# Leaky-form weight conversion, reciprocals by transposes, and one attention form for batches 1 to 3 in a fused attention and two-MLP kernel

## The chip, the cores and the metric

The kernel runs on one core of a Trainium2 chip. The metric is the device time of one execution in microseconds. The engines are TensorE (PE, with its weight loads as PEld), VectorE (DVE), ScalarE (ACT), GpSimd (POOL) and SyncE (SP), which issues most of the DMAs.

## The reference, cut to what matters

```python
def _attn_ref(q, k, v, g_q, g_k):            # (4, 12, 448, 64) each
    q_n, k_n = rmsnorm(q, g_q), rmsnorm(k, g_k)
    scores = np.matmul(q_n, k_n.transpose(0, 1, 3, 2)) / np.sqrt(64)
    attn = np.exp(scores - np.max(scores, axis=-1, keepdims=True))
    attn = attn / (np.sum(attn, axis=-1, keepdims=True) + 1e-09)
    return np.matmul(attn, v)

x = attn_out.transpose(0, 2, 1, 3).reshape(1792, 768)
x = (1 / (1 + np.exp(-(x @ w_gate)))) * (x @ w_val) @ w_out      # 768 -> 1536 -> 768
out = np.maximum(x @ w_in2, 0) ** 2 @ w_out2                     # 768 -> 2048 -> 768
```

The five weight matrices arrive as 64-bit floats, everything else as 32-bit floats.

## The kernel before

The four batches of 448 tokens pass one after the other through both MLPs (`sweep`, line 519). One pass walks over 68 weight blocks of 128x768: 24 of gate and value in turn, 12 of `w_out`, 16 of `w_in2`, 16 of `w_out2`. A product of 32-bit accuracy is made of three products of rounded operands, high by high, high by low and low by high (`mm3`, lines 508 to 512; lines 615 to 617 in the last stage). Only the first twelve blocks of the pass over batch 0 are multiplied in plain 32-bit form (line 539). High and low part of a block are made by `w_split`: ScalarE rounds (line 164), VectorE subtracts (line 165).

In the pass over batch 0 each block is first made from 64-bit words by `w_conv`: ScalarE scales the upper word, read as a 32-bit float (line 137), VectorE masks the sign bit in place (140), shifts the scaled word left by three and joins the sign (144), and joins the three top bits of the lower word (146). GpSimd then stores the 32-bit block to device memory (153), and the later passes load it from there (120). Three raw buffers and three converted ones make the ring; `w_ahead` sets how far loads, conversions and splits run ahead.

Batch 0's attention runs before the first pass, in an order written out by hand (`prologue`), and its end overlaps the first plain blocks. The attention of batch b+1 runs inside the pass over batch b: `slots_of` makes a list of small steps, which the main loop spreads evenly over the pass. Batches 0 and 1 use plain 32-bit products: scores per query chunk (`s_mm`), a maximum over two heads (`s_max`, line 268), exponentials, transposes of the probabilities (`c_mm`), products with V (`pv_mm`, line 313), and the reciprocals of the sums brought into the transposed layout by eight products with the identity per head pair (line 318). Batches 2 and 3 use the split form, the functions whose names end in 2: query and key are split into high and low parts (`a_hi`, `a_lo`), the halves that the other head's partitions need are copied by DMA (`a_dma`), scores take two products (line 398), the probabilities are normalised before the transposes (lines 425 to 430), split again behind them (`c_hi`, `c_lo`), and multiplied by a split V (lines 470, 472). A half is one head with two of the four query chunks; a batch has 24.

A scheduler then orders the instructions of each engine, and each engine runs its own queue in that order.

Of the kernel before, what the change touches and what calls it, by code (L numbers as in the profile page):

```python
# [8 lines left out]
F32 = mybir.dt.float32  # L9
# [8 lines left out]
def attention_moe_moe2_kernel(  # L18
# [104 lines left out]
    def w_conv():  # L123
# [183 lines left out]
    def pv_mm(st, o, rt):  # L307
# [330 lines left out]
    def slots_of(b):  # L638
# [5 lines left out]
        def do_s(key, c0):  # L644
            st = pairs[key]
            for c in (c0, c0 + 1):
                s_mm(st, c, att_tile())
            for c in (c0, c0 + 1):
                s_max(st, c)
                mid.append((s_exp, (st, c)))  # L650
            if c0 == 2:
                later(1, s_rec, st)

        def do_c(key, c):
            st = pairs[key]
            ps = att_tile().rearrange("p a (k c) -> p a k c", k=NF + 1)
            c_mm(st, c, ps[:, 0], ps[:, 1])
            c_copy(st, c, (act, act))

        def do_pv(key):  # L660
            st = pairs[key]
            ps = att_tile()
            pv_mm(st, ps[:, 0, :S], ps[:, 1, :S])
            for fn in (x_rec, x_sum, x_hi):
                mid.append((fn, (st,)))
            later(1, x_lo, st)
            later(1, lambda: pairs.pop(key))

        def do_a(key):
# [278 lines left out]
```

## Time and profile before

| | |
|---|---|
| median of three runs | 1309.39 us (1307.68 to 1309.93) |
| the profiled execution | 1309.2 us, span 1307.1 us |
| TensorE busy | 1284.9 us, 98% |
| VectorE busy | 938.4 us, 72% |
| ScalarE busy | 781.7 us, 60% |
| GpSimd busy | 130.3 us, 10% |

Shares are of the span. TensorE's matmuls are pipelined and their ends are modelled, so its busy time includes the tail of each; a stretch at 100% can still hold waits shorter than that tail. The span has the start-up (to 87 us), the pass over batch 0 (to 433), those over batches 1 (to 750), 2 (to 1047) and 3.

### The profile page before, as it was taken

To read this page: it belongs to the slowest core of one execution; us is meant where nothing else is said; L and a number is where in the kernel's file an instruction comes from. 1 tells how busy PE (TensorE), PEld (TensorE's weight loads), DVE (VectorE), ACT (ScalarE), POOL (GpSimd) and SP (SyncE) were. 2 spreads that over 40 slices of the span, in tenths; PEclk is the share of its full clock that TensorE was granted. 3 is DMA by queue.
4 is the path that set the end of the run, shared out by engine and by line. 5 is a ranking of instruction groups with operands and counts; after the bars stand their busy time and mean duration, and the time that the engine had idled before them with its cause. 6 is when DMAs were issued, how large, how long until landed. Compare 5 with 4: busy or idle time off the path is not lost.

```text
span 1307.1 us, 19338 instructions
## 1 busy us (share of the span) xinstructions
PE 1284.9 (98%) x6899; PEld 1120.1 (86%) x6899; DVE 938.4 (72%) x1643; ACT 781.7 (60%) x1600; POOL 130.3 (10%) x100
## 2 busy tenths in 40 slices
PE   8999999999899999999999999999999999999998
PEld 6554488788697999999999999999999999999998
DVE  6876999899898678768986478877897544435521
ACT  5764687568666678656664477765676455524421
POOL 3201214210221001000010000100010000000000
PEclk9999999999899999999999999999999999999999
DMA  5426897787788434333343533434324343333331
GB/s 144 103 76 216 273 292 246 252 270 218 245 232 273 130 113 121 105 114 107 107 113 105 146 97 110 125 100 114 99 86 121 116 127 109 109 109 109 108 114 46
DMA packets 155807, 189.62 MB, mean 145 GB/s; under 512 B 76096, under 2 KB 119616, under 8 KB 155712
## 3 DMA queue, kind: packets, MB, share of 16 engines
q1 hardware_dynamic: 148416, 161.19, 43.0%
q0 software_dynamic: 5440, 26.74, 5.0%
q8 instruction: 55, 0.90, 0.3%
q10 hardware_dynamic: 1856, 0.46, 0.2%
q14 instruction: 40, 0.33, 0.1%
HBM read 150.60 MB, written 32.24 MB: 140 GB/s over the span
## 4 chain that ended last, share of the span: by engine, by line
PE 73%; issue 10%; DVE 7%; DMA 4%; ACT 4%; POOL 2%; POOLq 0%; ACTq 0%; SPq 0%; DVEq 0%
PE acc L510 15%; PE acc L511 15%; PE acc L512 15%; PE acc L617 5%; PE acc L615 5%; PE acc L616 5%; PE att L398 3%; PE att L439 2%; DMA w<-wraw 2%; PE att L470 2%; POOL ms L232 1%; DVE nm L268 1%; PE att L472 1%; ACT p L280 1%; PE acc L313 1%
## 5 line engine op out<-in xcount | busy, mean ns | idle before, releaser
L165 DVE TENSOR_TENSOR wsp<-wraw,wsp 128x768 fp32r<-128x768 f32 x260 | 248.0, 954 | 130.8 <-ACT wsp L164 125.9
L510 PE MATMUL acc<-xy,wsp 128*128 128x448 f32 x888 | 326.7, 368 | 0.2 <-ACT rl L592 0.2
L512 PE MATMUL acc<-xy,wsp 128*128 128x448 f32 x888 | 326.1, 368 | 0.0
L511 PE MATMUL acc<-xy,wsp 128*128 128x448 f32 x888 | 325.9, 367 | 0.0
L164 ACT CAST wsp<-wraw 128x768 fp32r<-128x768 f32 x260 | 216.6, 834 | 130.9 <-PE acc L617 64.7
L512 PEld LDWEIGHTS acc<-xy,wsp 128*128 128x128 f32 x888 | 166.9, 188 | 16.1 <-issue 2.7
L510 PEld LDWEIGHTS acc<-xy,wsp 128*128 128x128 f32 x888 | 166.8, 188 | 16.1 <-issue 0.9
L511 PEld LDWEIGHTS acc<-xy,wsp 128*128 128x128 f32 x888 | 166.9, 188 | 15.0 <-issue 1.5
L232 POOL TENSOR_TENSOR ms<-ms,mhalf 112x16 f32<-112x16 f32 (+1 forms) x25 | 91.1, 3648 | 577.1 <-DVE ms L231 486.8
L616 PE MATMUL acc<-wsp,rb 128*128 128x384 f32 x384 | 129.2, 336 | 0.0
L617 PE MATMUL acc<-wsp,rb 128*128 128x384 f32 x384 | 129.0, 336 | 0.0
L615 PE MATMUL acc<-wsp,rb 128*128 128x384 f32 x384 | 128.8, 335 | 0.0
L510 PE MATMUL acc<-hb,wsp 128*128 128x448 f32 x288 | 106.2, 369 | 0.0
L511 PE MATMUL acc<-hb,wsp 128*128 128x448 f32 x288 | 105.5, 367 | 0.0
L512 PE MATMUL acc<-hb,wsp 128*128 128x448 f32 x288 | 105.5, 367 | 0.0
L417 ACT ACTIVATE p<-att,nm,ms 112x448 f32<-112x448 f32 x96 | 68.8, 724 | 34.7 <-DVE nm L408 34.5
L137 ACT ACTIVATE wraw<-raw 128x768 f32<-128x768 f32 x56 | 51.5, 920 | 51.8 <-DMA w<-wraw 27.8
L592 ACT ACTIVATE rl<-acc 128x448 f32<-128x448 f32 x64 | 35.0, 547 | 70.7 <-PE acc L512 69.9
L280 ACT ACTIVATE p<-att,nm 112x448 f32<-112x448 f32 x88 | 55.3, 639 | 33.7 <-DVE nm L268 32.3
L617 PEld LDWEIGHTS acc<-wsp,rb 128*128 128x128 f32 x384 | 72.1, 188 | 1.6 <-issue 1.3
L616 PEld LDWEIGHTS acc<-wsp,rb 128*128 128x128 f32 x384 | 72.1, 188 | 0.8 <-issue 0.7
L615 PEld LDWEIGHTS acc<-wsp,rb 128*128 128x128 f32 x384 | 72.1, 188 | 0.2
(136 smaller groups left out, 2167.7 us busy)
## 6 DMA issues: line engine op xcount, KB each, us to landing
wraw<-w SPq DMA_DIRECT2D x204, 384.0 KB, 3.0
w<-wraw POOLq DMA_DIRECT2D x56, 384.0 KB, 6.0
raw<-in_moe_w_out_dram SPq DMA_DIRECT2D x28, 768.0 KB, 5.4
raw<-in_moe_w_in_dram SPq DMA_DIRECT2D x16, 768.0 KB, 6.6
raw<-in_moe_w_gate_dram SPq DMA_DIRECT2D x12, 768.0 KB, 6.8
raw<-in_moe_w_val_dram SPq DMA_DIRECT2D x12, 768.0 KB, 6.1
out_dram<-ob SPq DMA_DIRECT2D x28, 192.0 KB, 2.9
qs<-qs SPq DMA_DIRECT2D x24, 224.0 KB, 3.0
```

What stands on the lines that cost most here:

```text
L137: size = nc.scalar.activation(out=t, in_=hi.bitcast(F32), func=AF.Copy, scale=2.0 ** -112)
L164: nc.scalar.copy(out=sp[:, 0], in_=t)
L165: nc.vector.tensor_tensor(out=sp[:, 1], in0=t, in1=sp[:, 0].bitcast(F32), op=ALU.subtract)
L232: nc.gpsimd.tensor_tensor(out=ms, in0=ms, in1=mhalf[:QR, 0:ms.shape[1]], op=ALU.pow)
L280: nc.scalar.activation(out=p[:, e], in_=ps[:QR, e, :S], func=AF.Exp, bias=nm[:, e:e + 1], scale=st["rq"][:, c, e:e + 1] if "rq" in st else ...
L417: nc.scalar.activation(out=p[:, i * (S + TAIL):i * (S + TAIL) + S], in_=ps[:QR, i, :S], func=AF.Exp, bias=nm[:, i:i + 1], scale=rq[:, 2 * ...
L510: nc.tensor.matmul(out=o, lhsT=wh, rhs=xh, start=start, stop=False)
L511: nc.tensor.matmul(out=o, lhsT=wh, rhs=xl, start=False, stop=False)
L512: nc.tensor.matmul(out=o, lhsT=wl, rhs=xh, start=False, stop=stop)
L615: nc.tensor.matmul(out=o, lhsT=rh, rhs=wh, start=(k1 == 0), stop=False)
L616: nc.tensor.matmul(out=o, lhsT=rh, rhs=wl, start=False, stop=False)
L617: nc.tensor.matmul(out=o, lhsT=rl, rhs=wh, start=False, stop=(k1 == K2 - 1))
```

## The change

Three edits. In `w_conv` ScalarE applies Prelu with slope 2^32 for negative values in place of a Copy: the slope adds 32 to the exponent of a negative word, and the shift by three moves that bit into the sign's place. VectorE then takes the three top bits of the lower word and joins them to the shifted word: two instructions instead of three. In `s_rec` GpSimd spreads the reciprocals over 64 columns per head, and four transposes replace the eight products of line 318; this form now serves batch 0 alone. In `slots_of` the plain branch goes, and batch 1 takes the split form, as do its first loads in the prologue.

```diff
-        size = nc.scalar.activation(out=t, in_=hi.bitcast(F32), func=AF.Copy, scale=2.0 ** -112)
+        size = nc.scalar.activation(
+            out=t, in_=hi.bitcast(F32), func=AF.Prelu, scale=2.0 ** -112, alpha=2.0 ** 32)
...
-        sign = nc.vector.tensor_scalar(
-            out=hi, in0=hi, scalar1=-(2 ** 31), scalar2=None, op0=ALU.bitwise_and)
+        low3 = nc.vector.tensor_scalar(
+            out=hi, in0=lo, scalar1=29, scalar2=None, op0=ALU.logical_shift_right)
...
         nc.vector.scalar_tensor_tensor(
             out=ti, in0=ti, scalar=3, in1=hi, op0=ALU.logical_shift_left, op1=ALU.bitwise_or)
-        nc.vector.scalar_tensor_tensor(
-            out=ti, in0=lo, scalar=29, in1=ti, op0=ALU.logical_shift_right, op1=ALU.bitwise_or)
...
         nc.vector.reciprocal(out=su, in_=su)
+        sb = st["sb"] = tmp_p.tile([128, 512], F32, tag="tmp", name="sb")[:QR].rearrange(
+            "p (c e d) -> p c e d", c=QC, e=2)
+        nc.gpsimd.tensor_copy(out=sb, in_=su.unsqueeze(3).to_broadcast([QR, QC, 2, D]))
...
         for c in range(QC):
-            for e in range(2):
-                nc.tensor.matmul(
-                    out=rt[e * D:(e + 1) * D, c * QR:(c + 1) * QR],
-                    lhsT=st["su"][:, c, e:e + 1].to_broadcast([QR, D]), rhs=ident[:QR, :QR],
-                    start=True, stop=True)
+            nc.tensor.transpose(
+                rt[:, c * QR:(c + 1) * QR], sb[:, c].rearrange("p e d -> p (e d)"), ident[:QR, :QR])
...
-        if b > 1:
-            for h in range(H):
...
         if b == 1:
-            add(lambda: do_stat((1, 0)))
+            add(lambda: do_stat((1, 0)), lambda: do_v((1, 0)))
             for _ in range(3):
                 add(lambda: None)
-            add(lambda: do_a((1, 0)))
-        for hp in range(HP):
-            key, nk = (b, hp), nxt(b, hp)
...
+            add(lambda: do_a2((1, 0)))
+        for h in range(H):
+            key, e = (b, h // 2), h % 2
...
```

The rest of `slots_of` behind this is the loop that batches 2 and 3 had, unchanged. How the scheduler's order moves, at three places:

VectorE, in the pass over batch 0, right behind the sixth gate-and-value pair's first product on VectorE (`L556`) in the kernel before; raw and wraw are the conversion's buffers, wsp the split block, su the sums of a softmax, nm its negated maxima:

```order
L556 TENSOR_TENSOR e<-acc,e 128x448
L287 TENSOR_SCALAR su<-su 112x8
L165 TENSOR_TENSOR wsp<-wraw,wsp 128x768
L146 SCALAR_TENSOR_TENSOR wraw<-raw_1432,wraw 128x768
L557 SCALAR_TENSOR_TENSOR e<-t,e 128x448
L288 RECIPROCAL su<-su 112x8
L140 TENSOR_SCALAR raw_1466<-raw_1466 128x768
L144 SCALAR_TENSOR_TENSOR wraw<-wraw,raw_1466 128x768
L165 TENSOR_TENSOR wsp<-wraw,wsp 128x768
L146 SCALAR_TENSOR_TENSOR wraw<-raw_1466,wraw 128x768
L559 TENSOR_TENSOR hb<-e,hb 128x448
```

The same stretch of that queue in the changed kernel, some instructions further on (`L141`, `L145` and `L164` are the two conversion steps and the split there; p and parts are the probabilities before and behind their transposes):

```order
L425 TENSOR_SCALAR su_1382<-su_1382 112x2
L145 SCALAR_TENSOR_TENSOR wraw<-wraw,raw_1563 128x768
L426 RECIPROCAL su_1382<-su_1382 112x2
L164 TENSOR_TENSOR wsp<-wraw,wsp 128x768
L430 TENSOR_SCALAR p<-p,su_1382 112x448
L430 TENSOR_SCALAR p<-p,su_1382 112x384
L430 TENSOR_SCALAR p<-p,su_1382 112x64
L457 TENSOR_TENSOR parts<-att,parts 128x3x224
L461 TENSOR_TENSOR parts<-att,parts 64x112 x2
L141 TENSOR_SCALAR raw_1614<-raw_1614 128x768
L405 TENSOR_REDUCE nm<-att 112x2
```

A conversion has lost its third row, and what stands between two conversions is now the normalising, splitting and maxima of the split attention.

TensorE, in the plain blocks (`L539`), before:

```order
L539 MATMUL acc<-xplain,wsp 128x448 x25
L244 MATMUL att<-ident,qk 128x112 x4
L539 MATMUL acc<-xplain,wsp 128x448 x6
L244 MATMUL att<-ident,qk 128x112 x4
L539 MATMUL acc<-xplain,wsp 128x448 x11
L262 MATMUL att<-kq 112x448 x4
L539 MATMUL acc<-xplain,wsp 128x448 x11
L295 MATMUL att<-ident,p 128x112 x7
L539 MATMUL acc<-xplain,wsp 128x448 x2
L295 MATMUL att<-ident,p 128x112 x7
```

and now (`L243` and `L398` prepare and multiply batch 1's first queries and keys):

```order
L539 MATMUL acc<-xplain,wsp 128x448 x33
L243 MATMUL att<-ident,qk 128x112 x4
L539 MATMUL acc<-xplain,wsp 128x448 x26
L398 MATMUL att<-ks,qs 112x448 x8
L539 MATMUL acc<-xplain,wsp 128x448 x8
L510 MATMUL acc<-xy_232,wsp 128x448
```

The two transposes of query and key have become one group, the plain score products have become two groups of four split ones, and the first transposes of probabilities have left the plain blocks.

TensorE again, where the pass over batch 0 meets that over batch 1 in the changed kernel (`L512` belongs to batch 1's first block):

```order
L512 MATMUL acc<-xy_1048,wsp 128x448
L439 MATMUL att<-ident,p 128x112 x6
L440 MATMUL att<-ident,p 128x112
L470 MATMUL att<-parts,vs 128x448
L472 MATMUL att<-parts,vs 128x448
L470 MATMUL att<-parts,vs 128x448
L472 MATMUL att<-parts,vs 128x448
L470 MATMUL att<-parts,vs 128x448
L472 MATMUL att<-parts,vs 128x448
L470 MATMUL att<-parts,vs 128x448
L398 MATMUL att<-ks,qs 112x448 x4
L510 MATMUL acc<-xy_1048,wsp 128x448
```

In the kernel before no attention step of batch 1 stands behind the first product of the pass over batch 1; here the last two steps with V and the transposes ahead of the last do, the products with V right behind these transposes.

## Rows read from the trace of the kernel before

**Rows 1.** windows: stretch, us, busy (count) of PE PEld DVE ACT POOL, PEclk, DMA share, GB/s

```profile
87.20:155.60 68.40, 67.07 (x231) 34.23 (x229) 50.73 (x76) 36.28 (x70) 13.13 (x14) 1.00 0.66 217
155.60:216.80 61.20, 57.65 (x314) 47.67 (x313) 59.82 (x87) 48.40 (x97) 12.74 (x14) 1.00 0.83 263
276.20:363.70 87.50, 83.87 (x443) 67.78 (x442) 80.78 (x127) 62.19 (x131) 12.23 (x18) 0.96 0.79 242
749.70:1047.30 297.60, 297.60 (x1613) 277.09 (x1612) 232.95 (x461) 193.56 (x409) 19.00 (x5) 1.00 0.38 109
1047.30:1307.10 259.80, 256.53 (x1323) 242.30 (x1320) 105.92 (x155) 105.37 (x188) 0.00 (x0) 1.00 0.34 104
```

**Rows 2.** timeline of DVE, three marking rows (start us, us, engine, line)

```profile
165.19 0.62 DVE L556 TENSOR_TENSOR e<-acc,e 128x448 f32<-128x448 f32 x1
...
367.56 0.61 DVE L593 TENSOR_TENSOR r<-rl 128x448 f32<-128x448 f32 x1
...
441.05 0.62 DVE L556 TENSOR_TENSOR e<-acc,e 128x448 f32<-128x448 f32 x1 [1.70 <-ACT p L417]
```

**Rows 3.** timeline of PE, start-up, plain blocks and first split block

```profile
56.19 3.23 PE L313 MATMUL acc<-pt,v 128*64 128x448 f32 x16
59.25 0.94 PE L318 MATMUL acc<-ident,su 112*64 112x112 f32 x16
...
131.69 1.76 PE L262 MATMUL att<-kq 64*112 64x448 f32 x8
...
141.75 0.84 PE L295 MATMUL att<-ident,p 112*128 112x112 f32 x7
...
155.58 0.71 PE L510 MATMUL acc<-xy,wsp 128*128 128x448 f32 x1
```

**Rows 4.** timeline of DVE, a full queue in the pass over batch 0

```profile
197.34 0.97 DVE L144 SCALAR_TENSOR_TENSOR wraw<-wraw,raw 128x768 int32<-128x768 int32 x1
198.21 0.58 DVE L140 TENSOR_SCALAR raw<-raw 128x768 int32<-128x768 int32 x1
198.68 0.64 DVE L331 TENSOR_TENSOR rs<-att,rs 128x448 f32<-128x448 f32 x1
199.21 0.97 DVE L146 SCALAR_TENSOR_TENSOR wraw<-raw,wraw 128x768 int32<-128x768 int32 x1
```

**Rows 5.** groups by form, 155 to 430 us (busy us, mean ns | idle before)

```profile
L137 ACT ACTIVATE wraw<-raw 128x768 f32<-128x768 f32 x52 | 47.8, 919 | 48.9 <-DMA w<-wraw 27.8 <-DVE wsp L165 15.0 <-issue 2.5
...
L268 DVE TENSOR_REDUCE nm<-att 112x2 f32<-112x896 f32 x22 | 23.8, 1083 | 0.0
...
L226 DVE TENSOR_REDUCE ms<-sq 112x8 f32<-112x512 f32 x10 | 6.8, 682 | 0.0
```

**Rows 6.** chain that ended last, one piece (start us, us, what)

```profile
436.47 0.82 PE att L398 x4
```

**Rows 7.** timeline of POOL, in the start-up and in stretch B

```profile
32.06 2.90 POOL L232 TENSOR_TENSOR ms<-ms,mhalf 112x16 f32<-112x16 f32 x1 [9.52 <-DVE ms L231]
...
222.16 7.65 POOL L232 TENSOR_TENSOR ms<-ms,mhalf 112x16 f32<-112x16 f32 x1 [0.72 <-DVE ms L231]
```

**Rows 8.** groups by form, 430 to 720 us, pass over batch 1

```profile
L457 DVE TENSOR_TENSOR parts<-att,parts 128x672 fp32r<-128x672 f32 x22 | 18.8, 854 | 4.2 <-ACT parts L452 3.9
...
L449 ACT CAST parts<-att 128x672 fp32r<-128x672 f32 x22 | 15.9, 724 | 6.3 <-PE att L440 6.0
...
L461 DVE TENSOR_TENSOR parts<-att,parts 64x112 fp32r<-64x112 f32 x44 | 12.0, 272 | 0.6
```

**Rows 9.** windows of core 0, around the clock's fall (columns as in 1)

```profile
336.00:340.00 4.00, 2.22 (x15) 1.73 (x13) 1.90 (x4) 2.52 (x6) 0.60 (x1) 1.00 1.00 325
340.00:344.00 4.00, 2.40 (x7) 1.60 (x9) 3.64 (x5) 3.19 (x6) 0.17 (x1) 0.56 0.40 161
```

More of the change, by code (lines that the diff above doesn't have):

```diff
@@ L315, in pv_mm @@
                     start=(kc == 0), stop=(kc == NF))
+        sb = st.pop("sb")
         for c in range(QC):
-            for e in range(2):
-                nc.tensor.matmul(
-                    out=rt[e * D:(e + 1) * D, c * QR:(c + 1) * QR],
-                    lhsT=st["su"][:, c, e:e + 1].to_broadcast([QR, D]), rhs=ident[:QR, :QR],
-                    start=True, stop=True)
+            nc.tensor.transpose(
+                rt[:, c * QR:(c + 1) * QR], sb[:, c].rearrange("p e d -> p (e d)"), ident[:QR, :QR])
         st["o"], st["rt"] = o, rt
@@ L642, in add @@
             slots.append(fns)
[L644 to L669, printed above, removed]
-            st = pairs[key]
-            ps = att_tile()
-            for i in range(2):
-                a_mm(st, i, ps[:, i])
-                a_copy(st, i)
         def do_load(key):
-            pairs[key] = (load_pair if key[0] < 2 else load_pair2)(*key)
+            pairs[key] = load_pair2(*key)
         def do_v(key):
-            (load_v if key[0] < 2 else load_v2)(pairs[key])
+            load_v2(pairs[key])
         def do_a2(key):
@@ L719, in do_stat @@
             later(2, stat_hat, st, 0)
[L720 to L748 removed]
         if b == 1:
[L750 removed]
+            add(lambda: do_stat((1, 0)), lambda: do_v((1, 0)))
             for _ in range(3):
                 add(lambda: None)
[L753 to L756 removed]
+            add(lambda: do_a2((1, 0)))
+        for h in range(H):
+            key, e = (b, h // 2), h % 2
+            nk = nxt(*key)
+            prev = ((b, (h - 1) // 2), (h - 1) % 2)
             more = nk[0] < B
@@ L760, in some @@
                 return [lambda: fn(nk)] if more else []
-            add(lambda key=key: do_s(key, 0), *some(do_load))
-            if hp:
-                add(lambda prev=prev: do_c(prev, QC - 1))
-                add(lambda prev=prev: do_pv(prev), *some(do_stat))
-            else:
-                add(*some(do_stat))
-            add(lambda key=key: do_c(key, 0))
-            add(lambda key=key: do_c(key, 1))
-            add(lambda key=key: do_s(key, 2))
-            add(lambda key=key: do_c(key, 2), *some(do_v))
-            if more:
-                add(*some(do_a if nk[0] < 2 else do_a2))
-        add(lambda: do_c((b, HP - 1), QC - 1))
+            add(lambda key=key, e=e: do_s2(key, e, 0), *(some(do_load) if e == 0 else []))
+            if h:
+                add(lambda prev=prev: do_c2(*prev, 1))
+            add(lambda key=key, e=e: do_s2(key, e, 1))
+            if e == 1 and more:
+                add(*some(do_a2))
+            if h:
+                add(lambda prev=prev: do_pv2(*prev))
+            if e == 0:
+                add(lambda key=key: do_c2(key, 0, 0), lambda key=key: split_v(pairs[key]), *some(do_stat))
+            else:
+                add(lambda key=key: do_c2(key, 1, 0), *some(do_v))
+        add(lambda: do_c2((b, HP - 1), 1, 1))
         add(lambda: None)
-        add(lambda: do_pv((b, HP - 1)))
-        add(lambda: None)
-        add(lambda: None)
+        add(lambda: do_pv2((b, HP - 1), 1))
         return slots
@@ L791, in load @@
         def load(i):
+            if i == HP:
+                pairs[keys[i]] = load_pair2(*keys[i])
+                return
             pairs[keys[i]] = load_pair(
@@ L819, in prologue @@
             at((-20, -11, -9.9, -8, -6, -4, 12)[i], load, i)
-            at(t - 1.5, stage, load_v, i)
             if i == HP:
                 continue
+            at(t - 1.5, stage, load_v, i)
             if i == 0:
```

27 lines of the change are left out of this document (1 added, 26 removed).

## Prediction

> **What bounds the kernel now.** I read the table of stretches first, since the mean shares hide the stages. The page gives TensorE 98% of the span, but a busy matmul there includes its pipeline's tail, so that share does not say that TensorE is short of time everywhere. [rows 1] cuts the span at the feed-forward stages: the plain blocks of token batch 0 (87.2 to 155.6), the rest of its gate and value blocks (155.6 to 216.8), its w_in stage (276.2 to 363.7), then the whole pass over batch 2 and the whole pass over batch 3. In 155.6 to 216.8 VectorE is busy 59.82 of 61.20 us, 97.7%, while TensorE is not full; in the pass over batch 2 TensorE is full and VectorE is at 78%. So only the pass over batch 0 (87 to 433 us), in which the weights are converted, can gain or lose from VectorE. Three instructions on VectorE's own timeline mark it [rows 2]: the sixth `L556` starts at 165.19, the sixteenth `L593` at 367.56, the thirteenth `L556`, which belongs to batch 1, at 441.05. I call 165.19 to 367.56 stretch B (202.4 us) and what follows to 441.05 stretch C (73.5 us). TensorE begins the first block behind the plain ones at 155.58 [rows 3], so at B's start VectorE is 9.6 us behind TensorE.
>
> **What an instruction costs in a full queue.** Neighbouring rows of VectorE start closer together than their durations: a scalar_tensor_tensor occupies 0.87 us (197.34 to 198.21), `L140` 0.47, a 448-element tensor_tensor 0.53 [rows 4]. I take 0.085 us off the mean duration of a row.
>
> **The conversion.** Before, one weight block costs 0.47 + 0.87 + 0.87 us on VectorE. The change drops `L146`. What takes `L140`'s place (a shift that reads the low word and writes the high one) is not in the trace; its nearest row is `L140` itself, also one source, one integer operation and the same strides, so 0.47; the other end is a two-source operation, 0.87. By the order, B holds 40, 39 and 40 of the three before, 87.5 us, and 43 of each of the two now, 57.6 us (74.8 at the other end). ScalarE's Prelu is not in the trace either; the Copy it replaces takes 0.92 us [rows 5]. The low end is the same; were it twice as long, ScalarE, idle 25.3 us in the 16 blocks of the w_in stage [rows 1], would still have 0.7 us per block left. I take no cost, and the order shows one table load in both kernels.
>
> **Batch 1's attention on VectorE.** The pass over batch 2 does all of batch 3's split attention, the last pass does none: 232.95 - 105.92 = 127.0 us [rows 1], less three look-ahead splits at 0.87, 124.4 us. The plain form: 24 maxima at 1.00, 12 reductions at 0.60, 12 scalings priced like them, 12 products and differences at 0.54, and 1.7 of small ones: 46.6 us [rows 4, 5]. By the order, B held 16 of the 24 maxima, so 31.1 us; now it holds 17 of the 24 halves, so 88.1 us. Splits (41 at 0.87, 35.7) and feed-forward work (31.0, now 31.6) hardly change. **B's queue on VectorE: 185.3 us before, 213.0 now.** That is a floor, since the queue keeps its order.
>
> **TensorE.** A plain score product costs 1.76/4 = 0.44 us, a plain value product 3.23/8 = 0.40, a transpose 0.84/7 = 0.12, the reciprocals of a pair 0.94 [rows 3]; a split product 0.82/4 = 0.205 [rows 6]. Four transposes in place of the reciprocals save 0.94 - 0.48 = 0.46 us a pair, five pairs before the plain blocks end the start-up 2.3 us earlier. In the plain blocks the attention goes from 36 transposes, 8 value products, 8 score products and one set of reciprocals (12.0 us) to 26 transposes, 8 value products and 8 split products (8.0): 4.0 us less, and TensorE is the limit there, VectorE being busy 50.73 of 68.40 [rows 1].
>
> **The copy on GpSimd** that feeds these transposes is new. Its nearest rows are GpSimd's 2.90 us for 112x16 [rows 7] and, as a lower bound, VectorE's 0.53 for 448 elements. By the order eight value products (3.23 us) stand ahead of the transposes in nearly every pair, so even 2.9 us is covered; without that cover it would cost up to 2.9 a pair, 17 us. The Trainium skill, GPSIMD Engine Reference, Elementwise, has 769 ns for a tight loop over 512 elements, an estimate of 0.8 us here; no row shows it.
>
> **The sum.** B starts when TensorE has done the plain blocks: 155.6 - 2.3 - 4.0 = 149.3, because VectorE's queue ahead of it, from the first `L556`, shrinks too (48 to 36 us by the order). At the 97.7% of the fullest stretch [rows 1] B lasts 213.0/0.977 = 218.0 us and ends at 367.3, 0.3 us earlier than now. In C TensorE sets the pace, as VectorE's 66 us of queue fit into it. Its attention there goes from 20.5 us (58 transposes, 8 score and 16 value products, two sets of reciprocals, 8 split products) to 19.2 (65 transposes, 56 split products): -1.3. New is a wait where the last transposes stand right ahead of the products that need them: a cast, a difference and two corner differences, 0.72 + 0.85 + 2 x 0.27 = 2.1 us [rows 8]. Twelve products of batch 1's third block now run earlier, -2.5. Last, TensorE can enter C with more lead: 9.6 us at B's start, 3.9 at its end (363.7 against 367.56); with VectorE the limit all through B I take half the difference, -3. So -0.3 - 1.3 + 2.1 - 2.5 - 3 = **-5.0 us**. The profiled execution took 1309.2 us around a span of 1307.1, 0.2 below the median of the three runs; 1309.2 - 5.0 = **1304.2 us**. Behind C nothing changes, TensorE being full there.
>
> **A rule that speaks against it.** GpSimd's 112x16 power takes 2.90 us at 32.06, with nothing on VectorE beside it, and 7.65 us at 222.16, in B [rows 7]; the stores behind it wait. The Trainium skill, SBUF — State Buffer, SBUF: two separate sides, says why it could be: GpSimd and VectorE share a pair of ports under an exclusive lock, which VectorE takes in two-port modes and, against a reading GpSimd operation, with two SBUF inputs. The trace agrees. The split form adds 48 one-source scalings in B; if each of four stores that a conversion waits for met one of up to 0.45 us, that estimate adds 1.8 us and the sum would be 1306.0.
>
> **Rivals.**
> *VectorE keeps its waits (slower).* In B it now spends 202.4 us on 185.3 of work, 91.5%; its attention steps wait in order for ScalarE, TensorE and GpSimd, and everything behind them waits too, the splits that TensorE needs first of all. At 91.5% B lasts 232.8, 14.8 more than in the sum: **1319.0 us**. It decides from 95.5%, where the 5.0 us are used up. For it: the split form has two more round trips per half than the plain one, and a starved TensorE loses its clock (granted 0.56 in 340 to 344, the lower level of 1.2 GHz for most of it, after it had idled 1.8 us of 336 to 340 [rows 9]). Against it: now B's waits are partly TensorE's own limit, and the full stretches run at 97.7%. Chance 0.26.
> *The two sides cancel.* Between 94.7 and 96.5% B is 1.9 us longer to 2.3 shorter than at that break-even: about **1309 us**. Chance 0.22.
> *The change does not do what it says:* the shift runs at the two-source price. Then B's floor is 230.2 and the sum gives 17.6 us more, **1321.8 us**. Against it: `L140` is as integer and as strided. Chance 0.04.
> *VectorE waits for nothing, or TensorE still sets the pace.* With no wait at all B lasts 213.0, **1299.2 us**; only if the split attention is cheaper than the difference of two passes does it fall further, at most to TensorE's own relief of about 15 us, 1294. Chance 0.03 beside the forecast.
>
> **How the numbers follow.** The forecast, a B between 96.5 and 100%, has 0.45. A measurement of this kernel tells changes over 0.2%, 2.6 us. Faster by more: 0.45 + 0.03 = 0.48; within: 0.22; slower: 0.26 + 0.04 = 0.30. The range runs from 1296, between no wait and TensorE's relief, to 1320, which takes in the slower rival and leaves out the slow shift. The forecast's own range is 1299.2 to 1306.9.
>
> **What would show it.** Right: `L140`'s successor at about 0.56 us, busy; VectorE above 95% from 150 to 365; plain blocks that end near 149; the first product of batch 1 near 428 instead of 433; later passes unchanged. Wrong: the shift near 0.95; the sixteenth `L593` after 375; TensorE idle for long before `L470` or `L398` in the pass over batch 0; a start-up that ends later than 87 us because transposes wait for GpSimd.

## The result, and the profile after

The changed kernel takes **1327.82 us** (median of 4 runs, 1323.76 to 1329.45) against 1308.54 for the kernel before on the same chip (1307.24 to 1309.93): a ratio of 1.0143, 95% interval 1.0114 to 1.0171. It is slower by 1.4%; the prediction of 1304.2 us, and its range to 1320, were wrong. The profiled execution took 1329.3 us around a span of 1327.5.

The table of stretches, cut at the same places of the work as [rows 1] (the columns are the same; batch 0's stages of w_out and w_out2 and the pass over batch 1 are left out here as there):

```profile
82.20:146.50 64.30, 62.78 (x197) 32.44 (x195) 40.56 (x65) 35.19 (x64) 13.75 (x15) 1.00 0.76 238
146.50:217.90 71.40, 60.63 (x307) 54.14 (x306) 67.21 (x132) 56.95 (x112) 11.26 (x14) 0.90 0.71 223
270.00:374.70 104.70, 86.39 (x421) 76.11 (x420) 98.67 (x196) 74.12 (x151) 15.52 (x20) 0.90 0.76 238
770.10:1067.70 297.60, 297.60 (x1613) 277.09 (x1612) 232.86 (x461) 193.40 (x409) 18.69 (x5) 1.00 0.38 109
1067.70:1327.50 259.80, 256.54 (x1323) 242.38 (x1321) 105.87 (x155) 105.31 (x188) 0.00 (x0) 1.00 0.34 104
```

TensorE reaches the plain blocks at 82.2 instead of 87.2 and needs 64.3 us for them instead of 68.4. Then the gain is lost: 71.4 us where there were 61.2, and 104.7 where there were 87.5, with a granted clock of 0.90 in both. The passes over batches 2 and 3 are as long as before, to a tenth. VectorE's busy share in the second row fell from 97.7% to 94.1% (67.21 of 71.40).

The three stretches that both tables leave out belong to the sum too. In the kernel before they were:

```profile
216.80:276.20 59.40, 56.48 (x306) 46.85 (x305) 52.13 (x76) 35.58 (x66) 19.17 (x15) 1.00 0.76 244
363.70:432.60 68.90, 68.43 (x428) 60.33 (x427) 55.91 (x80) 42.16 (x79) 12.19 (x13) 1.00 0.83 255
432.60:749.70 317.10, 317.10 (x1722) 295.93 (x1722) 237.09 (x470) 199.66 (x420) 21.96 (x6) 1.00 0.40 113
```

Now w_out lasts from 217.9 to 270.0 (52.1 us, 7.3 less), w_out2 from 374.7 to 445.5 (70.8 us, 1.9 more), and the pass over batch 1 from there to 770.1 (324.6 us, 7.5 more). Stage by stage, from the start-up on, the span changes by -5.0 - 4.1 + 10.2 - 7.3 + 17.2 + 1.9 + 7.5 = 20.4 us. So the plain blocks and the rest of the pass over batch 0 are 17.9 us longer together, and the pass over batch 1 adds 7.5.

VectorE's three marks, which answer to [rows 2]:

```profile
153.72 0.62 DVE L556 TENSOR_TENSOR e<-acc,e 128x448 f32<-128x448 f32 x1
...
383.35 0.62 DVE L593 TENSOR_TENSOR r<-rl 128x448 f32<-128x448 f32 x1
...
467.97 0.62 DVE L556 TENSOR_TENSOR e<-acc,e 128x448 f32<-128x448 f32 x1
```

Stretch B now starts at 153.72 and lasts 229.6 us (202.4 before); stretch C lasts 84.6 us (73.5 before). The same two stretches as windows:

```profile
153.72:383.35 229.63, 201.62 (x1017) 181.66 (x1016) 215.61 (x415) 167.12 (x327) 37.28 (x47) 0.93 0.76 238
383.35:467.97 84.62, 77.74 (x427) 72.47 (x426) 68.74 (x133) 54.09 (x105) 8.75 (x11) 0.94 0.64 195
```

and over the same marks of the kernel before:

```profile
165.19:367.56 202.37, 195.82 (x1052) 161.29 (x1051) 187.44 (x283) 142.67 (x287) 42.77 (x45) 0.98 0.79 248
367.56:441.05 73.49, 73.02 (x444) 64.19 (x443) 55.04 (x79) 43.93 (x82) 11.97 (x13) 1.00 0.82 247
```

VectorE works 215.61 us in B and 68.74 in C, 284.4 together; before it worked 187.44 and 55.04, 242.5 together, in 275.9 us. So from mark to mark VectorE has 41.9 us more to do, and the time from the first mark to the last grows by 38.4. The first mark comes 11.5 us earlier. The sum for the last mark is 41.9 - 3.5 (less idle) - 11.5 = 26.9 us later, of which 20.4 are left at the end: when that mark comes, TensorE is already 25 products into the third block of the pass over batch 1.

The marks are VectorE's own, and work has moved past them: over the whole kernel its busy time grows by 23.1 us only (938.4 to 961.5). C in particular reaches into the pass over batch 1. Up to TensorE's first product of that pass C lasts 62.2 us, before 65.0; behind it 22.5 us, before 8.5, because the last attention steps of batch 1 now run there (TensorE is busy 20.8 of these 22.5 us, at a granted clock of 0.92, and VectorE 14.4).

The prices were right. The groups by form, 140 to 430 us:

```profile
L145 DVE SCALAR_TENSOR_TENSOR wraw<-wraw,raw 128x768 int32<-128x768 int32 x54 | 51.0, 951 | 0.2
...
L137 ACT ACTIVATE wraw<-raw 128x768 f32<-128x768 f32 x53 | 48.2, 912 | 37.6 <-DMA raw<-in_moe_w_out_dram 11.1 <-DMA w<-wraw 8.4 <-DMA raw<-in_moe_w_in_dram 5.7
...
L141 DVE TENSOR_SCALAR raw<-raw 128x768 int32<-128x768 int32 x54 | 29.9, 559 | 8.5 <-ACT wraw L137 8.2
...
L430 DVE TENSOR_SCALAR p<-p,su 112x448 f32<-112x448 f32 x22 | 9.9, 448 | 0.3
```

The shift takes 559 ns, like the `L140` it was priced by, and the Prelu 912 ns, like the Copy it replaces [rows 5]. The copy on GpSimd takes 610 ns (6 of them, 3.7 us in all).

Where TensorE waits in the pass over batch 0, from the table of waits (us in total, times, longest us):

```profile
PE att L470 <- ACT p L417: 11.9, 3, 6.1
PE att L398 <- ACT p L417: 5.2, 2, 2.8
PE acc L615 <- ACT wsp L163: 3.6, 1, 3.6
PE att L243 <- DVE parts L461: 3.5, 1, 3.5
PE acc L510 <- ACT rl L592: 3.3, 3, 1.7
PE att L398 <- DMA qs<-qs: 2.9, 1, 2.9
```

Most of these rows are at an `att` tile of batch 1's attention. Here is the second longest single wait, on the timeline of three engines:

```profile
285.51 1.09 DVE L405 TENSOR_REDUCE nm<-att 112x2 f32<-112x896 f32 x1
...
288.07 0.15 DVE L408 TENSOR_TENSOR nm<-nm,ms 112x2 f32<-112x2 f32 x1
...
289.45 0.89 ACT L137 ACTIVATE wraw<-raw 128x768 f32<-128x768 f32 x1
...
290.37 0.72 ACT L417 ACTIVATE p<-att,nm,ms 112x448 f32<-112x448 f32 x1
...
291.08 0.71 ACT L417 ACTIVATE p<-att,nm,ms 112x448 f32<-112x448 f32 x1
...
291.94 0.74 PE L470 MATMUL att<-parts,vs 128*128 128x448 f32 x1 [4.85 <-ACT p L417]
...
292.48 0.57 PE L472 MATMUL att<-parts,vs 128*128 128x448 f32 x1
```

VectorE finishes the maxima of one half at 286.60 and multiplies them at 288.07, other steps of its queue lying between; ScalarE, in order, first does steps of the next keys and queries and a conversion step (289.45), and exponentiates from 290.37; TensorE, in order, stands for 4.85 us before `L470`, which needs the tile that exp has to free. The clock falls behind it:

```profile
182.00:287.00 105.00, 105.00 (x550) 96.17 (x548) 99.07 (x180) 77.98 (x145) 17.87 (x22) 1.00 0.77 246
287.00:290.50 3.50, 0.09 (x1) 0.00 (x0) 2.98 (x6) 3.40 (x7) 0.54 (x1) 1.00 1.03 332
290.50:308.00 17.50, 10.41 (x34) 8.58 (x35) 14.72 (x31) 8.10 (x18) 1.62 (x3) 0.51 1.08 330
```

From 182 to 287 TensorE is full at 2.4 GHz; it works 0.09 of the next 3.50 us, and from 290.5 to 308 it is granted 0.51, the lower level of 1.2 GHz for nearly all of that stretch, as after the idle in [rows 9].

### The profile page after: what moved, and what is told of

Same layout as the page of the kernel before. It is cut to its first block, busy times and chain, and to the rows that moved or that the text cites. A ratio compares the mean times of both kernels' runs of the same rounds, so it can differ in the third digit from the quotient of the medians.

```text
span 1327.5 us, 19239 instructions
## 1 busy us (share of the span) xinstructions
PE 1282.7 (97%) x6719; PEld 1139.3 (86%) x6719; DVE 961.5 (72%) x1809; ACT 810.0 (61%) x1648; POOL 124.9 (9%) x106
## 4 chain that ended last, share of the span: by engine, by line
PE 69%; DVE 7%; DMA 6%; issue 6%; ACT 3%; POOL 1%; ACTq 0%; DVEq 0%; POOLq 0%
PE acc L510 15%; PE acc L512 15%; PE acc L511 15%; PE acc L615 5%; PE acc L616 5%; PE acc L617 5%; PE att L398 3%; PE att L439 2%; PE att L470 2%; DMA raw<-in_moe_w_out_dram 2%; DVE wraw L145 1%; DMA raw<-in_moe_w_val_dram 1%; DMA raw<-in_moe_w_in_dram 1%; PE att L472 1%; DMA w<-wraw 1%
## 5 line engine op out<-in xcount | busy, mean ns | idle before, releaser
L164 DVE TENSOR_TENSOR wsp<-wraw,wsp 128x768 fp32r<-128x768 f32 x260 | 247.7, 954 | 124.7 <-ACT wsp L163 119.9
L512 PE MATMUL acc<-xy,wsp 128*128 128x448 f32 x888 | 326.1, 368 | 0.0
L511 PEld LDWEIGHTS acc<-xy,wsp 128*128 128x128 f32 x888 | 167.6, 189 | 13.7 <-issue 0.2
L512 PEld LDWEIGHTS acc<-xy,wsp 128*128 128x128 f32 x888 | 167.5, 189 | 13.7
L231 POOL TENSOR_TENSOR ms<-ms,mhalf 112x16 f32<-112x16 f32 (+1 forms) x25 | 82.8, 3315 | 593.9 <-DVE ms L230 459.9
L615 PE MATMUL acc<-wsp,rb 128*128 128x384 f32 x384 | 127.5, 337 | 3.7 <-ACT wsp L163 3.6
L417 ACT ACTIVATE p<-att,nm,ms 112x448 f32<-112x448 f32 x144 | 103.0, 722 | 40.1 <-DVE nm L408 39.4
L512 PE MATMUL acc<-hb,wsp 128*128 128x448 f32 x288 | 105.4, 367 | 0.0
L405 DVE TENSOR_REDUCE nm<-att 112x2 f32<-112x896 f32 x72 | 78.3, 1089 | 12.0 <-PE att L398 10.4
L398 PE MATMUL att<-ks,qs 128*112 128x448 f32 x288 | 74.0, 381 | 8.2 <-ACT p L417 5.2
L615 PEld LDWEIGHTS acc<-wsp,rb 128*128 128x128 f32 x384 | 72.2, 188 | 4.5 <-ACT wsp L163 3.8
L616 PEld LDWEIGHTS acc<-wsp,rb 128*128 128x128 f32 x384 | 72.4, 188 | 2.4 <-DVE wsp L164 2.3
```

The lines of the kernel that those rows point to most:

```text
L164: nc.vector.tensor_tensor(out=sp[:, 1], in0=t, in1=sp[:, 0].bitcast(F32), op=ALU.subtract)
L231: nc.gpsimd.tensor_tensor(out=ms, in0=ms, in1=mhalf[:QR, 0:ms.shape[1]], op=ALU.pow)
L398: nc.tensor.matmul(out=ps[:QR, i, :S], lhsT=st["qs"][:, e, z, c * QR:(c + 1) * QR], rhs=st["ks"][:, e], start=(z == 0), stop=(z == 1))
L405: nc.vector.tensor_reduce(out=nm, in_=st["s", e, c2][:QR, :, :S], axis=AX.X, op=ALU.max, negate=True)
L417: nc.scalar.activation(out=p[:, i * (S + TAIL):i * (S + TAIL) + S], in_=ps[:QR, i, :S], func=AF.Exp, bias=nm[:, i:i + 1], scale=rq[:, 2 * ...
L511: nc.tensor.matmul(out=o, lhsT=wh, rhs=xl, start=False, stop=False)
```

## The experiments

At the start there were two theories. **Theory V:** VectorE's queue in the pass over batch 0 sets its length, and the split form of batch 1 made the queue longer. **Theory A** (called **rival C** in the later runs): the split form holds the two `att` tiles until VectorE has read them, TensorE stands there and its clock falls, whatever VectorE's load. Every run was timed beside the kernel before on the same chip.

### The parts alone

**Conversion alone** (`e1_conv`), on the kernel before:

```diff
-func=AF.Copy, scale=2.0 ** -112
+func=AF.Prelu, scale=2.0 ** -112, alpha=2.0 ** 32
...
-out=hi, in0=hi, scalar1=-(2 ** 31), scalar2=None, op0=ALU.bitwise_and
+out=hi, in0=lo, scalar1=29, scalar2=None, op0=ALU.logical_shift_right
...
-nc.vector.scalar_tensor_tensor(
-    out=ti, in0=lo, scalar=29, in1=ti, op0=ALU.logical_shift_right, op1=ALU.bitwise_or)
```

> Kernel before with the conversion's edit alone (Prelu on ScalarE, low bits shifted out, one step of VectorE less for each tile); batch 1 stays in the plain form. Theory V (VectorE's queue sets the pass over batch 0, and the changed kernel was slower because that queue grew by about 28 us): here the queue shrinks by some 28 us, so the kernel comes out 5 to 12 us faster than before, until TensorE's own products hold the pass. Theory A (the split form holds the two att tiles until VectorE has read them, TensorE then stands and its clock falls): the plain form lets ScalarE free these tiles, so the pass was bound by TensorE already and the gain is 0 to 6 us; half-clock time stays under 10 us. Both theories: not slower.

Measured: 1295.14 us, ratio 0.9916 (0.9896 to 0.9937).

**Reciprocals alone** (`e2_rec`), on the kernel before:

```diff
+nc.gpsimd.tensor_copy(out=sb, in_=su.unsqueeze(3).to_broadcast([QR, QC, 2, D]))
...
-lhsT=st["su"][:, c, e:e + 1].to_broadcast([QR, D]), rhs=ident[:QR, :QR],
...
+rt[:, c * QR:(c + 1) * QR], sb[:, c].rearrange("p e d -> p (e d)"), ident[:QR, :QR])
```

> Kernel before with the reciprocals by transposes alone. The start of the first pass comes earlier by the 5.0 us that the changed kernel's trace shows less the part that the conversion brings, and each plain block by some 0.8 us: 2 to 6 us faster than before. If VectorE's queue sets the pass over batch 0 (theory V) half of this is lost again behind it; by theory A it all stays.

Measured: 1306.94 us, ratio 0.9987 (0.9974 to 1.0000), under what can be told from no change. The plain blocks start at 84.7 instead of 87.2, so the transposes bring the predicted 2.3 us there (2.5), and the pass over batch 0 gives them back.

**The split alone** (`e3_split`), the changed kernel with the old conversion and the old reciprocals:

```diff
-func=AF.Prelu, scale=2.0 ** -112, alpha=2.0 ** 32
+func=AF.Copy, scale=2.0 ** -112
...
-nc.tensor.transpose(
-    rt[:, c * QR:(c + 1) * QR], sb[:, c].rearrange("p e d -> p (e d)"), ident[:QR, :QR])
+lhsT=st["su"][:, c, e:e + 1].to_broadcast([QR, D]), rhs=ident[:QR, :QR],
```

> Changed kernel with the old conversion and the old reciprocals: batch 1 in the split form alone. Both theories put the loss in this part. Theory V: VectorE's queue in the pass over batch 0 is some 28 us longer still than in the changed kernel (old conversion), so the pass is longer by that: 1345 to 1365 us. Theory A: TensorE stands at the same att tiles, more often as VectorE is later still: 1335 to 1360 us, with half-clock time at or above the 44 us of the changed kernel. If the split were innocent, and the new conversion or the transposes the cause, this kernel would stand within 5 us of the kernel before.

Measured: 1363.54 us, ratio 1.0429 (1.0413 to 1.0445). Stretches B and C of this kernel, by its own marks (columns as in [rows 1]):

```profile
160.97:417.46 256.49, 215.07 (x1043) 185.78 (x1042) 252.07 (x463) 172.99 (x335) 38.86 (x46) 0.94 0.70 213
417.46:496.73 79.27, 69.81 (x366) 64.56 (x365) 73.15 (x133) 48.99 (x94) 8.95 (x12) 0.94 0.72 225
```

**All but the split** (`e4_conv_rec`), the kernel before with the edits of the first two runs together, batch 1 plain:

```diff
+func=AF.Prelu, scale=2.0 ** -112, alpha=2.0 ** 32
...
+nc.tensor.transpose(
+    rt[:, c * QR:(c + 1) * QR], sb[:, c].rearrange("p e d -> p (e d)"), ident[:QR, :QR])
```

> Kernel before with the conversion and the reciprocals, batch 1 in the plain form. Both theories: faster than before, about the sum of the two single edits, 7 to 16 us (1293 to 1302 us); theory A has it at the shorter end if the conversion alone gives little. If the two edits were what cost the changed kernel its 19 us, this one would be slower than before.

Measured: **1292.61 us**, ratio 0.9889 (0.9874 to 0.9904): faster than both kernels.

```profile
154.00:351.77 197.77, 195.49 (x1033) 159.93 (x1031) 165.11 (x252) 149.93 (x300) 39.45 (x51) 1.00 0.84 267
351.77:425.45 73.68, 70.86 (x411) 62.03 (x411) 44.10 (x61) 43.65 (x81) 9.01 (x12) 1.00 0.68 215
```

Two parts of the change are good together, nearly all of it by the conversion, and the third loses more than they gain: the split costs 1327.82 - 1292.61 = 35 us on top of the other two, and 55 us by itself. In the kernel without it TensorE works 195.49 of B's 197.77 us at full clock, so B is bound by TensorE. With the split and the old conversion VectorE works 252.07 of B's 256.49 us, 98.3%; there B is bound by VectorE. The changed kernel, at 93.9%, is neither, and both theories still fit it.

### VectorE's load, or the chain through the att tiles

**Less load, split form** (`e5_no_low`), the changed kernel with the conversion's two VectorE steps made one. It leaves out the three low bits that the weights' low word supplies:

```diff
-out=hi, in0=lo, scalar1=29, scalar2=None, op0=ALU.logical_shift_right
+out=ti, in0=ti, scalar1=3, scalar2=None, op0=ALU.logical_shift_left
...
-nc.vector.scalar_tensor_tensor(
-    out=ti, in0=ti, scalar=3, in1=hi, op0=ALU.logical_shift_left, op1=ALU.bitwise_or)
```

> Changed kernel with the conversion's two VectorE steps (shift of the low word, 0.56 us, and shift with OR, 0.95 us) replaced by one shift of about 0.5 us: it leaves out the three low bits of the weights' low word. VectorE's queue in the pass over batch 0 is some 40 us shorter (about 175 us instead of 212 between the two marks that the prediction uses); batch 1's attention, its two att tiles and their order stay as they are. Theory V (VectorE's queue sets the pass): that stretch falls from 229.7 us to TensorE's floor of about 198 us that the kernel without the split shows, the time to 1290 to 1300 us. Rival C (the att tiles, two instead of four banks at a time and freed late by the split's longer chain, hold TensorE whatever VectorE's load): the stretch stays above 215 us, the time above 1312 us, half-clock time stays near 40 us.

Measured: 1302.47 us, ratio 0.9955 (0.9942 to 0.9968). Taking the load away takes 25 us off with the attention's code untouched, but it stops 10 us above the kernel without the split, between the two expectations. (The profiled execution, from which the windows are, took 1299.08 us, the fastest of the ten.)

```profile
150.05:363.41 213.36, 199.63 (x1029) 180.10 (x1028) 182.16 (x373) 168.04 (x332) 38.80 (x47) 0.97 0.81 256
363.41:438.24 74.83, 72.66 (x420) 69.00 (x419) 59.52 (x122) 52.48 (x102) 8.30 (x10) 1.00 0.66 209
```

**Scalings on GpSimd** (`e8_norm_pool`):

```diff
-nc.vector.tensor_scalar(
+(nc.gpsimd if st["b"] == 1 else nc.vector).tensor_scalar(
     out=p[:, o0:o0 + n], in0=p[:, i0:i0 + n], scalar1=su[:, i:i + 1], scalar2=None, op0=ALU.mult)
```

> Changed kernel with batch 1's 72 scalings of the softmax rows (0.45, 0.41 and 0.25 us each) moved from VectorE to GpSimd. VectorE's queue is some 27 us shorter, by another piece than the conversion, and the scaling itself may take longer. Theory V: the stretch falls by 20 to 30 us if GpSimd keeps up, the time to 1298 to 1312 us. Rival C (the chain of the attention through the att tiles): GpSimd's slower scaling lengthens the chain, TensorE stands at the transposes of p, the time is unchanged or longer (1325 to 1350 us).

Measured: 1331.52 us, ratio 1.0172 (1.0145 to 1.0199). The groups by form, 154 to 390 us:

```profile
L430 POOL TENSOR_SCALAR p<-p,su 112x448 f32<-112x448 f32 x19 | 44.5, 2341 | 27.8 <-DVE su L426 20.1 <-PE acc L512 4.0 <-PE att L440 3.4
...
L141 DVE TENSOR_SCALAR raw<-raw 128x768 int32<-128x768 int32 x43 | 27.5, 643 | 6.1 <-ACT wraw L137 6.0
```

The run does not tell the theories apart: the 448-column scaling takes 2341 ns on GpSimd in place of 448 on VectorE, all three of a half some 4.8 us in place of 1.1, so it made the attention's chain longer while it made VectorE's queue shorter, and VectorE's shift went from 559 to 643 ns on average.

**More load, plain form** (`e10_repeat`), the opposite: the good kernel without the split, and VectorE made to do the shift again (the same values are written again):

```diff
+for _ in range(2 if i >= NPLAIN else 0):
+    nc.vector.tensor_scalar(
+        out=hi, in0=lo, scalar1=29, scalar2=None, op0=ALU.logical_shift_right)
```

> The kernel with the conversion's edit and the transposed reciprocals, batch 1 in the plain form (1292.6 us), in which the shift of the low word is done three times over instead of once in the conversions from the thirteenth on: VectorE gets some 50 times 2 times 0.56 us of work between the two marks, which brings its queue there to the changed kernel's 212 us, while batch 1's attention and its chain stay plain. Theory V (the queue's length alone): the stretch between the marks goes from 197.8 to 222 to 232 us, the time to 1317 to 1328 us, as slow as the changed kernel. Rival C (the split form's chain through the two att tiles adds its own standing of TensorE): the plain form at the same queue stays nearer to 215 to 220 us and 1308 to 1316 us, and what the changed kernel has beyond that is the chain's.

Measured: 1316.28 us, ratio 1.0050 (1.0032 to 1.0067). The load came to 202.1 us in B, not to the intended 212. Stretch (221.1 us) and time fall into the gap between the two expectations, so the run doesn't tell the theories apart.

**Products with v in an acc tile** (`e9_pv_acc`), on the changed kernel:

```diff
-o = st["o", e] = att_tile()[:, 0, :S]
+if st["b"] == 1 and not in_out2[0]:
+    o = st["o", e] = acc_tile()[:, :S]
+else:
+    o = st["o", e] = att_tile()[:, 0, :S]
...
```

> Changed kernel in which batch 1's products with v are summed in one of the four acc tiles, except in the stage of w_out2, instead of in an att tile: about 9 of batch 1's 66 uses of the two att tiles go away, among them those at which TensorE stood 11.9 us for exp. VectorE's queue is the same. Theory V: the time stays within 4 us of the changed kernel's 1327.8 us. Rival C: TensorE stands less and its clock falls less often: 1312 to 1322 us.

Measured: 1326.66 us, ratio 1.0135 (1.0098 to 1.0171): no difference from the changed kernel. The waits at `L470` are gone and others have come:

```profile
PE att L439 <- DVE p L430: 14.5, 2, 8.8
PE att L398 <- DMA qs<-qs: 5.7, 1, 5.7
```

It is not the clean test of the `att` tiles that it was meant to be, since TensorE's order has moved as well. Two groups of transposes of probabilities now stand in the plain blocks, and with them the wait of 8.8 us; the plain blocks take 84.5 us instead of 64.3, and from there to the pass over batch 1 it is 277.7 us instead of 299.0. What was gained in one place was lost in the other.

**Freeing steps sooner** (`e6_release`), on the changed kernel:

```diff
+def soon(st, fn, *args):
+    if st["b"] == 1:
+        with tc.high_priority(offset=200):
+            fn(st, *args)
...
-later(1, c_lo, st, e, c2)
+soon(st, c_lo, e, c2)
...
-later(1, pv_add, st, e)
+soon(st, pv_add, e)
```

> Changed kernel in which batch 1's VectorE steps that free an att tile (the maxima, the low parts of k, q and of the transposed p, the sum of the heads) are given a higher priority and are asked for a block sooner; the same instructions, some fifty of VectorE's 1695 rows in other places. Theory V: within 4 us of the changed kernel's 1327.8 us. Rival C: 1312 to 1322 us, less standing of TensorE at att tiles.

Measured: 1328.41 us, ratio 1.0147 (1.0110 to 1.0184). No effect to be seen, but a weak test: few steps changed places, and the longest wait at `L470` is still there.

### The two last runs

**Plain form with the shift repeated three times** (`e11_repeat3`), against the run that repeats it twice:

```diff
-for _ in range(2 if i >= NPLAIN else 0):
+for _ in range(3 if i >= NPLAIN else 0):
```

> As the run with the shift done three times over, but four times over: plain form of batch 1, VectorE with another 40 to 45 steps of 0.56 us between the two marks. That run had 202.0 us of VectorE work in a stretch of 221.0 us (kernel without the repeats: 165.1 in 197.8); this one should reach 215 to 222 us of work, the changed kernel's 215.7. Theory V: the stretch is 14 to 19 us longer than the work, 230 to 238 us, the time 1325 to 1336 us: the plain form is then as slow as the split form at the same load. Rival C: the split form's chain has its own part in the changed kernel's 229.7 us, so the plain form stays at 218 to 226 us, 1312 to 1322 us.

Measured: **1330.40 us**, ratio 1.0165 (1.0143 to 1.0188).

```profile
151.68:379.12 227.44, 207.12 (x1041) 163.09 (x1039) 208.38 (x360) 149.30 (x305) 46.25 (x48) 0.98 0.69 213
379.12:467.52 88.40, 80.73 (x433) 70.33 (x434) 77.88 (x142) 51.89 (x95) 13.64 (x17) 0.96 0.82 238
```

B's work came to 208.38 us, less than expected, and B lasts 227.4 us, between the two expectations; the time is in theory V's. C's work came to 77.88 us; over both, VectorE has 286.3 us of work in 315.8 us. The changed kernel has 284.4 in 314.2. With batch 1 in the plain form and as much work on VectorE between the marks, the kernel is as slow. TensorE's waits are other ones (its largest in the table of waits):

```profile
PE acc L618 <- ACT wsp L166: 7.4, 3, 3.5
PE att L300 <- ACT p L282: 5.8, 4, 2.7
PE acc L515 <- DVE wsp L167: 4.4, 7, 1.7
```

and its clock in B is 0.98 where the changed kernel's is 0.93. So neither the split form's `att` tiles nor the fallen clock is needed for such a length.

**Less load, and the products with v in an acc tile** (`e12_nolow_acc`), the edits of `e5_no_low` and `e9_pv_acc` together (the three low bits are left out here too):

```diff
-out=hi, in0=lo, scalar1=29, scalar2=None, op0=ALU.logical_shift_right
+out=ti, in0=ti, scalar1=3, scalar2=None, op0=ALU.logical_shift_left
...
-o = st["o", e] = att_tile()[:, 0, :S]
...
+    o = st["o", e] = acc_tile()[:, :S]
...
```

> Both edits at once on the changed kernel: the conversion's single shift (it leaves out the three low bits of the weights' low word) and batch 1's products with v summed in an acc tile outside the stage of w_out2. With VectorE's load down (182.1 us of work) the split form still had a stretch of 213.3 us and 1302.5 us, 10 us more than the kernel with the plain form. If the two att tiles hold TensorE in those 10 us: 1291 to 1298 us. If the cover is still VectorE's and ScalarE's queues in order (theory V): within 4 us of 1302.5 us.

Measured: 1292.24 us, ratio 0.9871 (0.9850 to 0.9892), 10 us less than `e5_no_low`. This is the first of the two expectations: here the edit that did nothing at the full load brings the rest. It also moves TensorE's steps (the first mark comes at 164.5, behind a wait for a scaling in the plain blocks), so whether the freed tile or the new order brings the 10 us stays open.

```profile
164.53:354.91 190.38, 188.77 (x1006) 172.76 (x1005) 173.14 (x353) 160.22 (x314) 39.40 (x42) 1.00 0.85 265
354.91:431.26 76.35, 75.94 (x442) 73.25 (x441) 60.07 (x121) 54.00 (x105) 9.62 (x13) 1.00 0.73 230
```

All runs side by side; work and length are the two windows of each kernel added up (B and C by its own marks), idle is their difference:

| kernel | batch 1 | first mark | VectorE's work | length | idle | time |
|---|---|---|---|---|---|---|
| conversion and reciprocals | plain | 154.0 | 209.2 | 271.5 | 62.2 | 1292.6 |
| conversion alone | plain | 156.6 | 207.6 | 269.9 | 62.3 | 1295.1 |
| before | plain | 165.2 | 242.5 | 275.9 | 33.4 | 1308.5 |
| reciprocals alone | plain | 162.5 | 244.5 | 278.4 | 33.9 | 1306.9 |
| shift repeated twice | plain | 150.0 | 255.0 | 295.5 | 40.5 | 1316.3 |
| shift repeated three times | plain | 151.7 | 286.3 | 315.8 | 29.6 | 1330.4 |
| less load, v in acc | split | 164.5 | 233.2 | 266.7 | 33.5 | 1292.2 |
| less load | split | 150.1 | 241.7 | 288.2 | 46.5 | 1302.5 |
| scalings on GpSimd | split | 154.3 | 273.2 | 316.1 | 42.9 | 1331.5 |
| v in acc | split | 166.7 | 273.5 | 300.9 | 27.4 | 1326.7 |
| changed kernel | split | 153.7 | 284.4 | 314.3 | 29.9 | 1327.8 |
| freeing steps sooner | split | 150.9 | 283.8 | 316.8 | 33.1 | 1328.4 |
| split alone | split | 161.0 | 325.2 | 335.8 | 10.5 | 1363.5 |

From 242 us of work upwards VectorE's idle time is 27 to 47 us in either form, and only at 325 us of work, where VectorE is busy 98.3% of B, does it fall to 10. But these marks take in more or less of the pass over batch 1 and of the plain blocks, kernel by kernel. The same is cleaner between two events on TensorE: its first plain block, and its first product of the pass over batch 1. "Behind" is the rest of the span, to its end:

| kernel | batch 1 | VectorE's work | length | idle | behind |
|---|---|---|---|---|---|
| conversion alone | plain | 248.8 | 331.2 | 82.4 | 874.5 |
| conversion and reciprocals | plain | 251.1 | 332.9 | 81.9 | 874.5 |
| before | plain | 299.4 | 345.4 | 46.0 | 874.5 |
| shift repeated twice | plain | 299.9 | 355.1 | 55.2 | 874.5 |
| reciprocals alone | plain | 301.7 | 347.7 | 46.1 | 874.6 |
| shift repeated three times | plain | 331.2 | 375.7 | 44.4 | 870.4 |
| less load | split | 265.3 | 338.8 | 73.5 | 877.3 |
| less load, v in acc | split | 267.6 | 333.3 | 65.7 | 875.7 |
| scalings on GpSimd | split | 306.0 | 364.8 | 58.8 | 880.1 |
| v in acc | split | 315.7 | 362.2 | 46.5 | 882.4 |
| changed kernel | split | 317.5 | 363.2 | 45.7 | 882.0 |
| freeing steps sooner | split | 317.7 | 364.2 | 46.4 | 881.5 |
| split alone | split | 373.0 | 395.9 | 22.9 | 875.9 |

Six of the eight kernels with 299 to 331 us of work, in both forms, have 44 to 47 us of idle time; the other two have 55 and 59. From the kernel before to the changed one the work grows by 18.1 us and the length by 17.9. So theory V holds for this part of the changed kernel. Of the 20.4 us, 17.9 are here, the start-up takes 5.0 back, and 7.5 lie behind: there the plain kernels need 870 to 875 us and the split ones 876 to 882. That the end of batch 1's attention, which runs over into a pass where TensorE is full, costs these 7.5 us is read from the trace and was not tried by itself.

The table also shows what is luck. The plain kernel with the shift repeated three times has 13.7 us more work in this part than the changed kernel, not the same, and is 12.4 us longer there; the two times agree because it needs 11.6 us less behind. The relation of work and length, which six of the eight kernels keep, does not rest on that pair.

Two things stay open. Rival C may still be true where VectorE's load is low (the 10 us between the two split kernels with less load). And all runs that change the load alone change it within the conversion, so they change its chain (load, Prelu, shift, join, split) along with VectorE's queue. Between 140 and 450 us the chain of work that ended last holds 74.3 us of DMA in the changed kernel, most of it loads of raw weight blocks, against 32.6 before and 72.2 in the plain kernel with three repeats. How much of VectorE's idle time is waiting for these loads, a run with a fourth raw buffer could show; there is none.

## Why the prediction was wrong, point by point

*Conversion, right.* Shift 0.56 us, Prelu 0.91 us, nothing hidden became visible; alone it brings 13 us. *The queue, right.* 213.0 us in B were worked out, 215.6 measured; 66 us in C, 68.7 measured. *Plain blocks, right:* -4.0 worked out, -4.1 measured. *The copy on GpSimd, right:* 0.61 us, between the bounds of 0.53 and 2.90 and under the estimate of 0.8; the start-up did not wait for it.

*Start-up, too small.* 2.3 us were worked out and 5.0 measured. The transposes alone bring 2.5 and all but the split 3.2. The other 1.8 us come with the split, though the split alone makes the plain blocks start 3.4 us later (90.6); why was not tried.

*B's start, wrong by 4.4 us.* The sum let VectorE's mark come together with TensorE's end of the plain blocks, at 149.3. TensorE was there at 146.5, but the mark came at 153.72, 7.2 us behind it; the lag of 9.6 us that the text itself had noted shrank by a quarter instead of vanishing.

***The step that failed* is "At the 97.7% of the fullest stretch B lasts 213.0/0.977 = 218.0 us".** One stage's share was carried over to the whole pass. VectorE's instructions wait in order for ScalarE and TensorE, and these waits did not vanish when the queue got longer. The sum left 5.0 us of idle time in B; there were 14.0, and 14.9 before (229.63 - 215.61 and 202.37 - 187.44). Over the plain blocks and the pass over batch 0 it was 46.0 us before and 45.7 after, and 44.4 in the plain kernel with three repeats. B took 229.6 us, 11.6 more than forecast: 9.0 by idle time and 2.6 by work. The rival "VectorE keeps its waits" had this mechanism, a B of 232.8 us and the break-even at 95.5%, with a chance of 0.26; it kept the share of idle time, where the idle time itself stayed. The text spoke against it with "the full stretches run at 97.7%"; but one stretch of 61 us did, and the w_in stage of the same rows was at 92.3% (80.78 of 87.50).

*C, wrong by 15.8 us.* The sum said: "In C TensorE sets the pace, as VectorE's 66 us of queue fit into it." VectorE's work did fit (68.74 of 84.6 us). But the terms of the sum (-1.3, +2.1, -2.5, -3) made C 68.8 us out of TensorE's work and 2.1 us of waiting, and TensorE was not busy for 6.9 us of C (0.5 before), 3.6 of them at `L615` for a conversion's cast, with a granted clock of 0.94 (1.00 before). The whole of C's growth lies behind TensorE's first product of the pass over batch 1 (22.5 us for 8.5), where the end of batch 1's attention had moved. How the 15.8 us divide among waits, clock and VectorE's lag behind TensorE is not shown. The true rival's 1319.0 us was still 8.8 us short, since it left B's start and C as forecast.

*Behind C, wrong by 6.5 us the other way.* "Behind C nothing changes": from the last mark to the end of the pass over batch 1 it is 302.1 us, before 308.7, as TensorE has run ahead of that mark.

*The rule that speaks against it, not seen.* GpSimd's 112x16 powers in B were to meet more of VectorE's scalings. They took 4.0, 2.9, 3.7 and 2.9 us there, and 5.3, 7.7, 4.5 and 3.0 in the kernel before.

The three differences are 4.4 + 11.6 + 15.8 = 31.8 us at the last mark; 6.5 of them did not reach the end. The 25.3 us that are left are what lies between the forecast's -5.0 and the span's +20.4.

The slow clock, which the rival named as an aid, is there (0.93 in B), but it isn't needed for B's loss: the plain kernel with three repeats has 0.98 there and as much idle time over the pass.

## What to carry to other kernels

When work is added to an engine that is nearly full in a loop where the engines wait for each other in order, keep its idle time in microseconds, not its best stretch's busy share: here some 46 us of idle time stayed while the work grew by 18. A change made of parts that pull the same engine both ways should be priced part by part: the conversion and the reciprocals brought 16 us, and the split, which relieves TensorE and loads VectorE where VectorE was nearly full, cost 35. Mark stretches by events of the engine that sets the end: between VectorE's own marks, past which work had moved, the same growth looked like 42 us. And an edit that does nothing under one bound (v in acc: 1 us) came with 10 us once that bound was lifted, by the freed tile or by the new order, so a failed relief is worth trying again after the bound has moved.

## What the runs showed of the hardware that was not expected

The same scaling of 112x448 that takes VectorE 448 ns takes GpSimd 2341 ns in the pass over batch 0, five times as long, while GpSimd's copy to 112x512 takes 610 ns; a price taken from one GpSimd row does not carry to another operation. In the run with the scalings on GpSimd VectorE's one-source shift went from 559 to 643 ns on average and its two-source step from 951 to 981. Taken apart by time (154 to 390 us), the 19 single shifts that overlap one of GpSimd's scalings take 754 ns on average and up to 1.61 us, the 20 others 557; the two-source steps take 1017 and 955. The Trainium skill, SBUF — State Buffer, section SBUF: two separate sides, says that GpSimd and VectorE share a pair of ports under an exclusive lock; these rows agree with it in direction. In the changed kernel itself, without scalings on GpSimd, the shift takes 559 ns.
